# x transposed by its loads, the product written over v, an early filter, a gate that passes through DRAM, and stores from one queue, in a kernel of a gated convolution and a local attention

## The chip, the core and the metric

The kernel runs on one core of a Trainium2 chip. Its engines work side by side and wait for one another through semaphores: TensorE (PE; its weight loads are shown as PEld), VectorE (DVE), ScalarE (ACT), GpSimd (POOL) and SyncE (SP). SP and ACT also issue DMAs; rows marked SPq and ACTq are these. The metric is device time in microseconds (us). Before the change it is 303.62 us, the median of three runs (303.6, 303.62, 306.52).

## The reference

All inputs are bf16. S = 2048 positions, D = 640 channels, H = 32 heads of 20 channels. x is `A_q`, and it serves both branches.

```python
x = A_q
g = sigmoid((x * gate_w).sum(-1, keepdims=True))
# branch a: a long convolution along S, by FFT
k_shift = sum over t of k_pad[:, t:t+S, :] * shift_k[:, 3-t]      # 4 taps
kv = k_shift * v
y  = irfft(rfft(kv padded to 2S) * rfft(ssm_k padded to 2S))[:S] + kv * ssm_D
a  = x * y
# branch b: attention with 8 keys per query, at distances 0, 2, 4 .. 14
q, k, v = split(x @ wqkv)
b  = (softmax(q . k[i - 2w] / sqrt(20)) @ v[i - 2w]) @ wo
out = g * a + (1 - g) * b
```

## The kernel before

**Order of work.** Every piece of work is a Python generator that yields requests (class `Req`: engine, estimated cost, dependencies, PSUM slots). A planner (`Plan.run`) takes them one by one by estimated start time and priority, and the instructions are emitted in that order. So each engine has a fixed order of instructions that rests on the planner's estimates; at run time an engine that waits holds all that stands behind it. PSUM is four slots of two banks. A request with engines "AD" may go to ACT or DVE, whichever the estimates say ends first.

**Layout.** Positions are held by parity: even ones first, then odd ones, so that the dilation of 2 becomes neighbourhood. `xT` is x with channels on the partitions (five blocks of 128).

**Stages, with their names in the profile's rows.**

1. *Loads* (`loads`, L339; all on SP) and small ones on ACT's queue (`heads`, L388): the tap weights `wraw` and the halo of k, both in the tile `early`. x comes as `xS`, and `transposes` (L451) turns it: 80 PE transposes (trx, L458), copied to `xT` by DVE and ACT.
2. *Projections.* `vproj` (L467): 18 units of 10 matmuls (psv, L476), copied to VW. `qkproj` (L507): five column blocks of q and of k, three units of 10 matmuls each (pj, L522), copied to a staging tile `stg`; one to three units make a block's q, three more its k. `fragger` (L541) moves 20-row pieces of `stg` (fragments) by DMA to `qb` and `kb`.
3. *Gate* (`gate`, L487): 160 matmuls of one column (gps, L494), whose weights are strided columns of `xT` in two halves, so that the result stands in the layout of the end. Then an exponential, a reciprocal, and `g_nat` and `omg` (1 - g).
4. *Short convolution* (`conv`, L418): on DVE, four rounds (conv 0 to 3) of 7 operations and a product with v (L443). The product goes to a tile `pv` in another order, from there to DRAM (`kv_d`) once all rounds are done, and back as `kvT` (`kv_back`, L694) with positions on the partitions.
5. *Attention*: eight sets of four heads. Per set five groups of score matmuls (sc, L589), exponentials on ACT (L597, into ETall), 72 products with v (O, L617), normalization on DVE (L626, L629). Three pairs of `kb`/`qb` take turns, so a set's fragments can be moved only when the set three before it has been scored.
6. *Long convolution.* Two steps of a transform (L653 and L669, each followed by copies on ACT or DVE) in two halves of the channels, for the filter (`h`, tile Hs) and for the product (`u`, tile U). `mults` (L750) multiplies them on DVE, with Hs and with Hw, a copy of Hs whose partition halves are swapped by DMA (`swaps`, L734). `inverse1` (L767): ten units of 16 matmuls per half (i, L777), copied to Cm.
7. *Output projection* (`outproj`, L788): oT copies of transposed attention output, then 16 units (op, L810), scaled by `omg` on ACT into bl.
8. *End* (`final`, L841): six units. Each has up to 96 matmuls (i, L859), two copies on ACT (yb, L866), a product and an addition on DVE (L871, L873), and four stores (L876), two issued by SP and two by ACT.

The second swap waits for the last reader of kvT, since its tile takes kvT's place:

```python
yield Req("S", 1.0, outs("h", P) + [ev("p3")] + ([ev("us1")] if P else []))
```

and the stores take turns on two queues:

```python
(nc.sync, nc.scalar)[gg % 2].dma_start(raw(outf, ...), reg[32 * gg:32 * gg + 32])
```

## Time and profile before

| what | value |
|---|---|
| median of three runs | 303.62 us |
| profiled execution: its time, its span | 305.58 us, 303.8 us |
| granted PE clock, mean | 0.844 |
| busy: PE, DVE, ACT | 231.9, 172.5, 177.8 us |
| transposes of x: first start | 10.9 us |
| psv units: first start | 14.2 us |
| gate matmuls | 8.94 us, up to 63.3 us |
| first scores | 63.3 us |
| last O ends | 166 us |
| second swap, issue to landing | 238.5 to 253.2 us |
| last addition on DVE ends | 300.5 us |

A page shows one profiled execution. Busy time is a sum over stages with different limits, so what an edit is worth has to be read in its own stage. Three views are used. The *chain* follows the work that ended last back from the end: each row has its start, its length and what it is (engine, tile, line, number of instructions). The *waits* say who waited for whom: microseconds in total, number of times, the longest. The *timeline* has instructions in order of time; the bracket at a row's end is idle time before it and what ended it ("issue": nothing that the profile shows). The trace also holds a record of every DMA packet with its size and time, and the order of a program's instructions on each engine can be read off the built program.

### The profile page before, as it was taken

How to read it: one execution, taken by the hardware profiler on the slowest of the kernel's cores; microseconds unless marked ns; L12 is line 12 of the kernel's file. 1: busy time of each engine (PE TensorE's matmuls, PEld its weight loads, DVE VectorE, ACT ScalarE, POOL GpSimd, SP SyncE). 2: the span in 40 equal slices, each digit the busy share in tenths (PEclk: the TensorE clock that was granted, in tenths of full speed). 3: DMA queues.
4: the chain of work that ended last, by engine and by line, in shares of the span. 5: the costliest groups of instructions: out<-in, count | busy, mean ns of one | idle time of the engine just before them, and what ended most of it. 6: DMA issues, size and time to landing. Idle time of an engine off the chain costs nothing.

```text
span 303.8 us, 8436 instructions
## 1 busy us (share of the span) xinstructions
PE 231.9 (76%) x3781; PEld 185.7 (61%) x3786; DVE 172.5 (57%) x181; ACT 177.8 (59%) x217; POOL 24.5 (8%) x23
## 2 busy tenths in 40 slices
PE   0499999997988895994888979999999742984210
PEld 0399888965655564563566868889877732973100
DVE  0138999993724334243766999996006656804443
ACT  0146553248368884596977898767756750773240
POOL 9920170000000000001000000000000000000000
PEclk9999999859799799697555999999999795895555
DMA  6982983402166569868993194001990490002343
GB/s 198 321 328 82 371 301 65 127 2 53 25 174 228 147 125 157 139 115 192 281 211 64 25 234 95 2 2 41 202 239 8 100 230 19 2 2 69 77 119 86
DMA packets 36985, 39.92 MB, mean 131 GB/s; under 512 B 23383, under 2 KB 32215, under 8 KB 35798
## 3 DMA queue, kind: packets, MB, share of 16 engines
q1 hardware_dynamic: 34480, 36.78, 48.6%
q10 hardware_dynamic: 2470, 2.62, 3.5%
q8 instruction: 29, 0.48, 0.7%
q14 instruction: 6, 0.05, 0.1%
HBM read 23.49 MB, written 5.24 MB: 95 GB/s over the span
## 4 chain that ended last, share of the span: by engine, by line
PE 58%; DVE 17%; DMA 9%; ACT 6%; SPq 4%; issue 4%; ACTq 1%; DVEq 0%
PE pj L522 14%; PE i L777 9%; PE psv L476 9%; PE op L810 7%; PE O L617 5%; DVE U L269 5%; DVE Hs L269 4%; DMA Hw<-Hs 4%; DMA xS<-in_A_q_dram 3%; PE sc L589 3%; PE gps L494 3%; SPq L563 2%; PE s L669 2%; DMA kb<-stg 2%; DVE qg L871 2%
## 5 line engine op out<-in xcount | busy, mean ns | idle before, releaser
L597 ACT ACTIVATE ETall<-sc 121x912 bf16<-121x912 f32 (+1 forms) x80 | 63.4, 858 | 22.2 <-PE sc L589 21.9
L522 PE MATMUL pj<-xT,Wqk 128*128 128x342 bf16 (+1 forms) x300 | 56.0, 342 | 2.8 <-ACT ETall L597 1.9
L522 PEld LDWEIGHTS <-Wqk 128*128 128x128 bf16 x300 | 30.6, 106 | 20.9 <-issue 3.2
L777 PE MATMUL i<-F,Hs 128*128 128x128 bf16 x160 | 27.2, 251 | 8.6 <-DVE Hs L760 8.6
L777 PEld LDWEIGHTS <-Hs 128*128 128x128 bf16 x160 | 26.0, 183 | 9.0 <-DVE Hs L760 8.8
L267 ACT CAST Cm<-i 128x1024 bf16<-128x1024 f32 x20 | 20.2, 1012 | 17.5 <-PE i L777 17.5
L476 PE MATMUL psv<-Wv,xT 128*121 128x320 bf16 x180 | 28.7, 313 | 1.0 <-DVE xT L269 1.0
L269 DVE CAST U<-s 128x1024 bf16<-128x1024 f32 (+2 forms) x23 | 25.8, 1171 | 6.0 <-PE s L669 3.2
L589 PE MATMUL sc<-qb,kb 31*128 31x114 bf16 x576 | 20.2, 243 | 10.7 <-DMA kb<-stg 3.7
L777 PE MATMUL i<-F,Hw 128*128 128x128 bf16 x160 | 27.1, 252 | 1.3 <-DVE Hw L763 1.3
L777 PEld LDWEIGHTS <-Hw 128*128 128x128 bf16 x160 | 26.0, 183 | 1.5 <-DVE Hw L763 1.5
L267 ACT CAST stg<-pj 128x684 bf16<-128x684 f32 (+1 forms) x21 | 15.6, 745 | 18.7 <-PE pj L522 14.3
L476 PEld LDWEIGHTS <-xT 128*121 128x121 bf16 x180 | 24.9, 142 | 2.5 <-issue 1.2
L267 ACT CAST Hs<-s 128x960 bf16<-128x960 f32 (+1 forms) x25 | 23.1, 994 | 3.1 <-PE s L669 1.8
L589 PEld LDWEIGHTS <-kb 31*128 31x128 bf16 x576 | 11.6, 104 | 20.5 <-issue 14.4
L669 PEld LDWEIGHTS <-G 64*128 64x128 bf16 x512 | 20.9, 103 | 4.4 <-issue 2.7
L269 DVE CAST Hs<-s 128x1024 bf16<-128x1024 f32 (+2 forms) x17 | 19.1, 1152 | 7.6 <-PE s L653 6.1
L810 PE MATMUL op<-wo,oT 128*128 128x512 bf16 (+1 forms) x155 | 22.6, 301 | 0.3
L267 ACT CAST VW<-psv 121x640 bf16<-121x640 f32 x18 | 12.5, 696 | 14.6 <-PE psv L476 14.6
L866 ACT CAST yb<-i 128x960 bf16<-128x960 f32 (+1 forms) x12 | 9.9, 873 | 18.0 <-DVE qg L873 16.8
L810 PEld LDWEIGHTS <-oT 128*128 128x128 bf16 x160 | 16.5, 147 | 5.9
L269 DVE CAST stg<-pj 128x726 bf16<-128x726 f32 (+1 forms) x9 | 8.0, 899 | 21.2 <-PE pj L522 14.6
(57 smaller groups left out, 331.2 us busy)
## 6 DMA issues: line engine op xcount, KB each, us to landing
Hw<-Hs SPq DMA_DIRECT2D x8, 640.0 KB
xS<-in_A_q_dram SPq DMA_DIRECT2D x4, 640.0 KB
kin<-in_A_k_dram SPq DMA_DIRECT2D x2, 1280.0 KB
vin<-in_A_v_dram SPq DMA_DIRECT2D x2, 1280.0 KB
kv_d<-pv SPq DMA_DIRECT2D x4, 640.0 KB
h_lin<-in_A_ssm_k_dram SPq DMA_DIRECT2D x8, 320.0 KB
kvT<-kv_d SPq DMA_DIRECT2D x8, 320.0 KB
qg<-in_A_q_dram SPq DMA_DIRECT2D x4, 640.0 KB
```

The source lines that it names most:

```text
L267: nc.scalar.copy(dst, src)
L269: nc.vector.tensor_copy(dst, src)
L476: nc.tensor.matmul(ps[0:BK, n0 // 320, 0:320], lhsT=xT[:, dt, s0:s0 + BK], rhs=Wv[:, dt, n0:n1], start=(dt == 0), stop=(dt == NDT - 1))
L494: nc.tensor.matmul(gps[64 * hh:64 * hh + 64, t:t + 1], lhsT=raw(a, X0 + 16 * hh + t, [a.ap[0], [32, 64]]), rhs=wg[:, dt:dt + 1], start=(dt ...
L522: nc.tensor.matmul(ps[:, i, 0:n], lhsT=Wqk[:, dt, w, 128 * ft:128 * ft + 128], rhs=xT[:, dt, s0:s0 + n], start=(dt == 0), stop=(dt == NDT ...
L589: nc.tensor.matmul(scs[rg // 2][:, rg % 2, BQ * bb:BQ * bb + BQ], lhsT=kb[r:r + DH + NF, BK * b:BK * b + 128], rhs=qb[r:r + DH + NF, BQ * ...
L597: nc.scalar.activation(st["ET"][0:BK, e, :, 0:BQ * nb], scs[k][0:BK, :, 0:BQ * nb], ACT.Exp, scale=SCALE)
L617: nc.tensor.matmul(O[:, (b - b0) // 6, c0:c0 + 21], lhsT=st["ET"][0:BK, e, hh, BQ * bb:BQ * bb + 128], rhs=VW[0:BK, b, 4 * t + h4, :], sta ...
L669: nc.tensor.matmul(ps[:, c, 160 * jj:160 * jj + 160], lhsT=st["G"][rows, j0 + jj, rr, :], rhs=Am[rows, :, 2 * (j0 + jj) + rr, :], start=(r ...
L777: nc.tensor.matmul(o, lhsT=src[:].rearrange("p q (j c) l -> p c l (q j)", c=2)[:, c, l + il, :], rhs=M[:, k, :], start=(k == 0), stop=(k = ...
L810: nc.tensor.matmul(op[:, n0:n1], lhsT=oT[:, ft].rearrange("p h m a -> p a (h m)")[:, t, :], rhs=wo[:, ft, n0:n1], start=(ft == 0), stop=(f ...
L866: nc.scalar.copy(yb[:, 0:m, 320 * k:320 * k + 320].rearrange("p n (q c) -> p q n c", q=2), pss[k][:, :, 0:160 * m].rearrange("p q (n c) -> ...
```

## The change

Six edits go together.

1. **x.** The four loads of x are now transposing DMAs, straight from DRAM into `xT`. `xS`, the 80 transposes and their copies are gone. Wq and Wk are loaded between the x loads; the tap weights and the halo move from ACT's queue to SP's, behind x. A q or k unit now waits only for the x loads that it reads.
2. **The convolution product** is written over v (`vin`) instead of into `pv`, and each round's part is stored as soon as it is done (`kv_out`). `kv_d` is now a plain position-by-channel array, and `kv_back` reads it in runs of 80 channels.
3. **The filter** `h_lin` has a tile of its own from the start and its loads wait for nothing of the convolution. The tags of several later tiles change places ("H" and "kv"), and the second Hw takes the tile of the first Hs, so the second swap waits for the first half's inverse (`i10`) instead of kvT's last reader.
4. **Gate.** 80 matmuls with contiguous weights; the result, by position, goes to DRAM (`g_scr`) and comes back in the layout of the end by four loads.
5. **Planner.** ACT gets a handicap of 600 (`LEAN_QK`) for the copies of q and k, scores take one PSUM slot at a time, and the estimate of an inverse unit rises. ETall is set to one only in its last 128 columns.
6. **Stores.** All 24 are issued by SP.

In the built program the planner orders the first part anew: 14 psv and 10 pj units stand before the first scores (18 and 7, and the gate, before), and one projection unit instead of three stands before the first inverse units. More copies of q and k go to DVE, and one of the five oT copies to ACT.

```diff
 LAT = {("P", "A"): 230.0, ("P", "D"): 230.0, ("A", "P"): 120.0, ("D", "P"): 120.0, ("A", "D"): 100.0, ("D", "A"): 100.0}
 SWITCH = 110.0
+LEAN_QK = 600.0
...
-        return min((self.start(r, e) + self.cost(r, e), self.start(r, e), e) for e in r.engs)
+        found = []
+        for e in r.engs:
+            s = self.start(r, e)
+            found.append((s + self.cost(r, e) + (r.lean if e == "A" else 0.0), s, e))
+        end, s, e = min(found)
+        return s + self.cost(r, e) if s < INF else INF, s, e
 
     def run(self):
         while self.streams:
...
-    xS = p0.tile([128, 16, D], BF, name="xS", tag="oS")
-    pv = p0.tile([128, 4, 2, 16, 80], BF, name="pv", tag="kv")
+    h_lin = p0.tile([128, 80, 2, 64], BF, name="h_lin", tag="kv")
-    kv_d = dpool.tile([4, 128, 2, 16, 80], BF, name="kv_d")
+    kv_d = dpool.tile([S, D], BF, name="kv_d")
+    g_scr = dpool.tile([S], F32, name="g_scr")
+    g_pos = p0.tile([128, 16], F32, name="g_pos")
...
         def load_x(c):
-            yield from load(f"x{c}", xS[:, 4 * c:4 * c + 4, :], xq4[:, c // 2, 4 * (c % 2):4 * (c % 2) + 4, :], 1900.0)
+            g = yield Req("S", 500.0, (), move=2600.0)
+            nc.sync.dma_start_transpose(xT[:, :, X0 + 512 * c:X0 + 512 * c + 512],
+                                        raw(x2, (1024 * (c % 2) + c // 2) * D, [[2 * D, 512], [1, D]]))
+            mark(f"x{c}", g)
+
+        def load_rows(name, dst, src, r0, r1, deps=(), bg=1500.0):
+            yield from load(name, dst, raw(src, r0 * D, [[16 * D, 128], [1, (r1 - r0) * D]]), (r1 - r0) * 128 * 1280 / 250.0, deps, bg)
...
-            yield from load_rows(f"v{a}", v_[:].rearrange("p n c -> p (n c)"), v2, 8 * a, 8 * a + 8, () if a else [ev("xS")])
-
-        yield from load("ident", ident[:], ca["ident"].ap(), 100.0)
+            yield from load_rows(f"v{a}", v_[:].rearrange("p n c -> p (n c)"), v2, 8 * a, 8 * a + 8, ())
+
         yield from load_x(0)
-        yield from load("Wv", Wv[:], W3[:, :, 2, :], 2400.0)
+        yield from load("Wv", Wv[:], W3[:, :, 2, :], 2600.0)
         yield from load_x(1)
+        yield from load("W0", Wqk[:, :, 0, :], W3[:, :, 0, :], 2600.0)
         yield from load_x(2)
+        yield from load("W1", Wqk[:, :, 1, :], W3[:, :, 1, :], 2600.0)
         yield from load_x(3)
+        yield from load("wraw", wraw.rearrange("p c j -> p (c j)"), raw(A_shift_k, 0, [[0, 128], [1, 4 * D]]), 2200.0)
+        for a, b in ((1, 113), (113, 128)):
+            yield from load(f"halo{a}", halo[a:b].rearrange("p n c -> p (n c)"), raw(k2, (16 * a - 3) * D, [[16 * D, b - a], [1, 3 * D]]), 900.0)
         yield from load_k(0)
-        yield from load("W0", Wqk[:, :, 0, :], W3[:, :, 0, :], 2400.0)
         yield from load_v(0)
-        yield from load("W1", Wqk[:, :, 1, :], W3[:, :, 1, :], 2400.0)
         yield from load_k(1)
         yield from load_v(1)
+        yield from load("ident", ident[:], ca["ident"].ap(), 200.0)
...
-        for q in range(4):
-            yield from load(f"kvD{q}", kv_d[q].rearrange("p c n i -> p (c n i)"), pv[:, q].rearrange("p c n i -> p (c n i)"), 3000.0, [ev("conv")], 1500.0)
-        h_lin = p0.tile([128, 80, 2, 64], BF, name="h_lin", tag="H")
-        st["h"] = h_lin
                 yield from load(f"h{q}{c}", h_lin[32 * q:32 * q + 32, :, c, :],
-                                raw(A_ssm_k, (160 * q + 80 * c) * S, [[64, 32], [S, 80], [1, 64]]), 2100.0, [ev("conv")], 1500.0)
+                                raw(A_ssm_k, (160 * q + 80 * c) * S, [[64, 32], [S, 80], [1, 64]]), 2100.0, (), 1500.0)
+    def kv_out():
+        for a in range(16 // CR):
+            n = CR * a
+            g = yield Req("S", 500.0, [ev(f"conv{a}")], move=2600.0)
+            nc.sync.dma_start(raw(kv_d[0:1, 0:1], n * D, [[16 * D, 128], [1, CR * D]]),
+                              st["vin"][n // 8][:, n % 8:n % 8 + CR, :].rearrange("p n c -> p (n c)"))
+            mark(f"kvD{a}", g)
+
+    def load_G():
+        yield Req("S", 1.0, [ev("conv")])
         G = p0.tile([128, 32, 2, 128], BF, name="G", tag="G")
         st["G"] = G
         for a in range(4):
-            yield from load(f"G{a}", G[:, 8 * a:8 * a + 8], cf["G"].ap().rearrange("p (a r b) -> p a r b", a=32, r=2)[:, 8 * a:8 * a + 8],
-                            1300.0, [ev("conv")], 1500.0)
+            g = yield Req("S", 500.0, [ev("kvD3")], move=2000.0, bg=1500.0, pri=1)
+            nc.sync.dma_start(G[:, 8 * a:8 * a + 8], cf["G"].ap().rearrange("p (a r b) -> p a r b", a=32, r=2)[:, 8 * a:8 * a + 8])
+            mark(f"G{a}", g)
...
-        nc.scalar.dma_start(wraw.rearrange("p c j -> p (c j)"), raw(A_shift_k, 0, [[0, 128], [1, 4 * D]]))
-        for a, b in ((1, 113), (113, 128)):
-            nc.scalar.dma_start(halo[a:b].rearrange("p n c -> p (n c)"), raw(k2, (16 * a - 3) * D, [[16 * D, b - a], [1, 3 * D]]))
...
-        nc.gpsimd.memset(ETall[:], 1.0)
+        nc.gpsimd.memset(ETall[:, :, :, 3 * BQ:], 1.0)
...
-        yield Req("D", 2500.0, [Ev(12000.0)])
+        yield Req("D", 2500.0, [ev("wraw")])
...
-            yield Req("D", c0, [ev(f"k{half}")])
+            yield Req("D", c0, [ev(f"k{half}"), ev("halo113")])
...
-            nc.vector.tensor_tensor(pv[:, :, :, n:n + CR, :].rearrange("p q c n i -> p n (q c) i"),
-                                    pa[:].rearrange("p n (x i) -> p n x i", i=80),
-                                    st["vin"][half][:, r:r + CR, :].rearrange("p n (x i) -> p n x i", i=80), ALU.mult)
+            v_ = st["vin"][half][:, r:r + CR, :]
+            nc.vector.tensor_tensor(v_, pa[:], v_, ALU.mult)
             mark(f"conv{a}", g)
...
-    def transposes():
...
-                        nc.tensor.transpose(tr[:, dd, 128 * k:128 * k + 128], xS[:, 4 * c + k, 128 * (d0 + dd):128 * (d0 + dd) + 128], ident[:, :])
...
-        return [ev(f"xT{c}{d}") for d in (0, 4)]
+        return [ev(f"x{c}")]
...
-        g = yield Req("P", 160 * 28.0, xdeps(3) + xdeps(1) + [ev("vproj")], take=1, mode="c", mm=160)
+        g = yield Req("P", 80 * 28.0, xdeps(3) + xdeps(1) + [ev("vproj")], take=1, mode="f", mm=80)
...
-                a = xT[:, dt, 0:1]
-                for hh in range(2):
-                    nc.tensor.matmul(gps[64 * hh:64 * hh + 64, t:t + 1], lhsT=raw(a, X0 + 16 * hh + t, [a.ap[0], [32, 64]]), rhs=wg[:, dt:dt + 1],
-                                     start=(dt == 0), stop=(dt == NDT - 1), tile_position=(0, 64 * hh), skip_group_check=True)
+                nc.tensor.matmul(gps[:, t:t + 1], lhsT=xT[:, dt, X0 + 128 * t:X0 + 128 * t + 128], rhs=wg[:, dt:dt + 1],
+                                 start=(dt == 0), stop=(dt == NDT - 1), skip_group_check=True)
...
-        nc.scalar.activation(g_nat[:], gps[:], ACT.Exp, scale=-1.0)
+        nc.scalar.activation(g_pos[:], gps[:], ACT.Exp, scale=-1.0)
+        r = yield Req("S", 500.0, [r.done], move=2500.0)
+        nc.sync.dma_start(g_scr[:].rearrange("(t p) -> p t", p=128), g_pos[:])
+        for gg in range(4):
+            r = yield Req("S", 500.0, [r.done], move=200.0)
+            nc.sync.dma_start(g_nat[32 * gg:32 * gg + 32, :], raw(g_scr[0:1], HS * (gg % 2) + 16 * (gg // 2), [[32, 32], [1, 16]]))
+        r = yield Req("D", 200.0, [r.done])
         nc.vector.tensor_scalar(omg[:], g_nat[:], -1.0, 1.0, ALU.mult, ALU.add)
...
-                    g = yield Req("P", 10 * (n / 2.4 + 2.5), xdeps(3) + xdeps(1) + [ev(f"W{w}")], take=1, mode="f", mm=10)
+                    need = {2 * (c // 3) + e for c in (2 * k, 2 * k + 1) for e in range(min(1, (342 * (c % 3) + 341) // 512) + 1)}
...
-                    r = yield Req("AD", n=m, deps=deps, give=g.banks)
+                    r = yield Req("AD", n=m, deps=deps, give=g.banks, lean=LEAN_QK)
...
-                g = yield Req("P", 4 * nb * 28.0 + 30.0, [ev(f"set{t}"), ev("ET")], take=2, mode="s", mm=4 * nb)
-                scs = []
...
+                    g = yield Req("P", 2 * nb * 28.0 + 30.0, [ev(f"set{t}"), ev("ET")], take=1, mode="s", mm=2 * nb)
+                    sc = psum(g, "sc")
...
-        yield Req("G", 1.0, [ev("xS"), ev("conv1")])
+        yield Req("G", 1.0, [ev("conv1"), ev("kvD1")])
...
-        Hs = p0.tile([128, 4, 64, PL], BF, name="Hs", tag="kv")
+        Hs = p0.tile([128, 4, 64, PL], BF, name="Hs", tag="H")
         st[("h", 0)] = Hs
...
-                g = yield Req("S", 500.0, [ev("p2")] + [ev(f"kvD{q_}") for q_ in range(4)], move=1500.0, bg=1500.0)
-                nc.sync.dma_start(st["kvT"][32 * q:32 * q + 32, c].rearrange("p (b n) i -> p b (n i)", b=4),
-                                  kv_d[q, :, c].rearrange("(a b) n i -> a b (n i)", b=4))
+                g = yield Req("S", 700.0, [ev("p2")] + [ev(f"kvD{a}") for a in range(4)], move=2000.0, bg=1500.0)
+                nc.sync.dma_start(st["kvT"][32 * q:32 * q + 32, c], raw(kv_d[0:1, 0:1], 160 * q + 80 * c, [[64 * D, 32], [D, 64], [1, 80]]))
         mark("kvT", g)
...
-        U = p0.tile([128, 4, 64, PL], BF, name="U1", tag="H")
+        U = p0.tile([128, 4, 64, PL], BF, name="U1", tag="kv")
...
-            yield Req("S", 1.0, outs("h", P) + [ev("p3")] + ([ev("us1")] if P else []))
-            Hw = st["p3"].tile([128, 4, 64, PL], BF, name="Hw", tag="Hw") if P == 0 else st["p2"].tile([128, 4, 64, PL], BF, name="Hw", tag="kvT")
+            Hw = st["p3"].tile([128, 4, 64, PL], BF, name="Hw", tag="Hw") if P == 0 else p0.tile([128, 4, 64, PL], BF, name="Hw", tag="H")
             st[("w", P)] = Hw
...
-                    r = yield Req("P", 16 * 64.0 + 30.0, [ev(f"m{P}{c}{l0}")], take=1, mode="f", mm=16)
+                    r = yield Req("P", 16 * 82.0 + 30.0, [ev(f"m{P}{c}{l0}")], take=1, mode="f", mm=16)
...
-        oT = p0.tile([128, NDT, 2, 64, 16], BF, name="oT", tag="H")
+        oT = p0.tile([128, NDT, 2, 64, 16], BF, name="oT", tag="kv")
...
-        yb2 = p0.tile([128, 2, 3, D], BF, name="yb2", tag="H")
+        yb2 = p0.tile([128, 2, 3, D], BF, name="yb2", tag="kv")
...
-                (nc.sync, nc.scalar)[gg % 2].dma_start(raw(outf, (32 * (gg // 2) + gg % 2 + 2 * t0) * D, [[64 * D, 32], [2 * D, m], [1, D]]),
+                nc.sync.dma_start(raw(outf, (32 * (gg // 2) + gg % 2 + 2 * t0) * D, [[64 * D, 32], [2 * D, m], [1, D]]),
                                                        reg[32 * gg:32 * gg + 32])
```

## The prediction

> **What bounds the kernel now.** I read the engine totals, then the chain that ended last, then the table of waits, then single stretches of the timeline. The page:
>
> ```profile
> span 303.8 us, 8436 instructions
> PE 231.9 (76%) x3781; PEld 185.7 (61%) x3786; DVE 172.5 (57%) x181; ACT 177.8 (59%) x217; POOL 24.5 (8%) x23
> PE 58%; DVE 17%; DMA 9%; ACT 6%; SPq 4%; issue 4%; ACTq 1%; DVEq 0%
> ```
>
> PE has most of the chain, but no engine is full for the whole span: the stages end on different things. The chain in order of time (start, length, what):
>
> ```profile
> 1.16 9.72 DMA xS<-in_A_q_dram
> 10.93 1.90 PE trx L458 x16
> 12.86 1.24 DVE xT L269
> 14.22 4.81 PE psv L476 x20
> ...
> 54.39 8.94 PE gps L494 x145
> ...
> 118.16 3.08 DMA kb<-stg
> 121.29 0.56 PE sc L589 x12
> ...
> 242.10 11.11 DMA Hw<-Hs
> 253.33 1.76 DVE Hs L760
> ...
> 278.82 0.97 ACT yb L866
> 279.82 1.17 DVE qg L871
> 281.01 1.17 DVE qg L873
> 282.20 0.38 ACTq L876
> 282.62 0.44 ACTq L876
> 283.28 0.73 issue
> 284.01 0.97 ACT yb L866
> ```
>
> Rows are taken at the full clock (0.844 is granted in the mean). Five places: x arrives late and is turned on PE; the gate is 8.94 us of PE before the first scores (63.3); the score sets then wait for fragments; the second swap leaves PE and DVE idle; and in the tail ACT stands behind its own stores, with a period of 5.19 us (278.82 to 284.01). The waits (total, times, longest) and a PE row of the tail:
>
> ```profile
> ACT yb L866 <- DVE qg L873: 16.8, 5, 3.4
> DVE Hs L760 <- DMA Hw<-Hs: 5.8, 1, 5.8
> ```
> ```profile
> 274.99 1.62 PE L859 MATMUL i<-Cm,T 32*32 32x160 bf16 x128 [1.87 <-issue]
> ```
>
> **Start, up to the first scores.** The 80 transposes, 0.89 us per 16, and their copies go. What x costs instead, no row shows. Below: the four plain x loads, 512 pieces of 1280 B at 58 ns over 16 DMA engines, 1.9 us each. Above: the same elements as 2-byte pieces, 327,680 at the 9 ns of the gate-weight load, 184 us. Between them: runs of 256 B, 2,560 pieces at the 18 ns of the identity's load, 2.9 us. I take 2.9, the row nearest to a load that reads whole runs of 128 columns; the upper end belongs to the slow rival below.
>
> The Trainium skill, "VectorE: DVE Perf Modes", section on the three transpose paths, speaks against the change: it gives the DMA path 1309 ns for 128x128, which for 20 blocks is an estimate of 26 us a load. "Advanced Engine Details and Errata", section X-Bar Transpose (TRN2), says instead that such DMAs run at about 90% of a plain copy. No row here decides between them; by the first page's figure the sum below would come to about 367 us, by the second's to what I forecast.
>
> Before, the tap weights (38.6 us of engine time, 2.4 us over 16) and the halo rode ACT's queue beside x; now they stand behind x on SP's. First data came 1.7 us after its issue. Adding in queue order from 2.4 us: x0 5.3, Wv 8.2 (2.3, and 0.5 for ACT's small loads), x1 11.1, Wq 13.4, x2 16.3, Wk 18.6, x3 21.5, taps 23.9, halo 25.7, k 28.8; about 1.2 more until a consumer starts. PE starts at 9.4, not 10.9, and has no wait for x3 (23 us). The new order has 14 psv units (1.36 us) and 10 pj units (1.47) before the first scores: 9.4 + 19.0 + 14.7 = 43.1, against 63.3. ETall cannot be set before the halo is read, near 37; its memset took 6.35 us for 7,520 columns, so 1.7 for 2,048, and the exponentials are not held. The gate comes later: 80 contiguous matmuls at the transposes' 56 ns (same 128x128 weights) are 4.5 us, against 8.94.
>
> **What is late next: DVE.** The convolution's first operation, at 25.7 before, waits for taps, halo, k and two staging copies now: 31.4. Conv 0 takes 12.4 us, conv 1 12.1, one staging copy 0.9 (a bank is held until then), 16 operations of 1.49 and the first two sets' normalizations (2.7 each) follow: conv 3 ends near 86, against 83.5. Writing the product over v costs the same 1.49. The third block's k staging (0.9) stands behind it on DVE, and behind that on SP four kb fragments (0.75 each) and about 2.5 us to land: the fourth set's scores start at 92.7 instead of 106.7. PE and ACT can serve three sets by then (first at 43, second at 67 after the gate, third near 79; a set is 8.6 us of exponentials), so DVE sets this date: 14 us gained. Bounds: 5, if PSUM banks held for DVE stop PE as well, and 20, where the second set already stands.
>
> From the fourth set on the order keeps its shape: the fifth set's last kb fragment still stands behind two q fragments that wait for the fourth set's scores (118.16 above). The lead stays 14 us up to the last O, at 166 before. More staging copies on DVE and the filter loaded early (four stage-1 units go into that gap) I put at zero: ACT has 76 us of work in 110 there.
>
> **Through DRAM.** Product stores: same size, free of conv's end. Reading them back now takes 16,384 pieces of 160 B; between 13 ns (the filter's 128 B) and 18 ns (256 B) that is 13.3 to 18.4 us, against 12.6 now. The last piece landed at 163.1, first use is 172.1: 9 us of cover, and the cost is what exceeds it. The gate's store, 2,048 pieces of 4 B at 9 ns, is 1.2 us, 7.4 at 58 ns; its values are used some 80 us later. But its store waits on SP for DVE's reciprocal, with the fifth set's q fragments behind it, and the four loads add 0.5 us of SP each: zero to 3 us. Zero taken.
>
> **Output projection and first inverse.** One projection unit instead of three now stands before the first inverse units, and ACT makes one of the five oT copies: PE waits for the first two products (1.74 each). Dates: op 199.0 to 200.4, products ready 201.5, ten inverse units of 1.31 to 214.7, fifteen of 1.40 to 235.7, against 233.6. Cost 2.1.
>
> **Second swap.** Its tile no longer waits for the last reader of kvT but for the first inverse, so it is issued near 215, beside 21 us of projection; it needs 13 (238.54 to 253.2). DVE's 5.8 us wait goes; next is DVE's own cast at 247.5. If the clock stays at full speed, up to 0.8 more.
>
> **Tail.** ACT no longer queues behind the stores. DVE's two operations, 2.35 us, would be the period, but PE is next: 128 matmuls run in 1.6 us and then wait for issue, 3.46 us from page to page (274.99, 278.45). By that, units 1 to 5 end on PE at 275.7, 278.8, 280.0, 283.0 and 283.4; adding ACT's 1.82 and DVE's 2.35 in turn, the last addition ends at 288.65 instead of 300.53: 11.9. SP issues four stores one after the other where two queues shared them, 0.85 later at the end. Net 11.0; 8 if store bandwidth binds (384 pieces of 96 ns over 16 engines are 2.3 us per unit).
>
> **Sum**, against the profiled execution's span: 303.8 - 14 + 2.1 - 5.8 - 11.0 = 275.1. Its execution took 305.58, so 276.9; the median, 303.62, lies 2.0 below that execution: 275.
>
> **Rivals.** *The early gain is lost:* DVE's convolution, SP's in-order waits and the fragments give back most of the 14, and swap and tail alone stay: 303.6 + 2.1 - 5.8 - 11.0 = 289. For it: DVE starts conv 5.7 us later; against: the set dates above.
> *The tail stays slow:* instruction issue or stores keep some 4 us of period: 281. For it the 1.87 rows; against, the 3.46 pitch.
> *PE and ACT gain more:* sets at the pace of exponentials, 268.
> *Slower: the transposing loads.* The change does turn x in the DMA, but in short pieces. If a load writes 32 bytes per partition at a time, 20,480 pieces at the 9 ns that the smallest take are 11.5 us. Everything behind x waits four times the excess: 4 x (11.5 - 2.9) = 34, so 275 + 34 = 309, slower by 1.8%. It decides from 2.9 + 28.5/4 = 10 us a load. For it: the smallest pieces' price; against: the x data here are whole 1280 B rows.
>
> **How the numbers follow.** Forecast 0.55 (270 to 282), early gain lost 0.14, slow tail 0.10, more gain 0.09, slow transposes 0.12 (300 to 340, a quarter of it within 1%). A measurement of this kernel tells about 1% from no change. Faster by over 1%: 0.88; slower by over 1%: 0.09; within: 0.03. Range 264 to 294: it takes in the bounds 5 and 20 of the lead and the first three rivals, and leaves out the slow transposes.
>
> **What would show it.** First psv near 9.5 and no trx rows; first scores near 43, fourth set near 93; gps about 4.5 us; no wait of DVE Hs on Hw<-Hs; ACT yb waits for PE, not for qg, and yb rows 2.4 to 3.5 us apart. It is wrong if psv units wait for x beyond 25 us, if scores wait for kb beyond the dates given, or if the stores' landing sets the end.

## The result, and the profile after

The changed kernel takes **283.19 us** (median of 281.92, 282.81, 283.58 and 284.1) against 305.07 us for the kernel before on the same chip: a ratio of 0.927, with a 95% interval of 0.918 to 0.936. The forecast was 275.0 with a range of 264 to 294. Ratios, here and below, compare the executions in the faster of two states that the record tells apart, while a median takes in all of them, so a ratio can differ a little from the quotient of two medians. The profiled execution took 281.92 us, its span is 280.1 us, and the sum had said 275.1.

The head of the page of the changed kernel: span, busy times, and the shares of the chain by engine.

```profile
span 280.1 us, 8105 instructions
PE 224.8 (80%) x3622; PEld 179.5 (64%) x3626; DVE 175.6 (63%) x186; ACT 169.0 (60%) x204; POOL 20.2 (7%) x23
...
PE 59%; DVE 12%; ACT 10%; DMA 8%; issue 5%; SPq 3%; ACTq 1%; DVEq 0%
```

No engine's busy time moved by more than 9 us (PE 231.9 to 224.8, ACT 177.8 to 169.0, DVE up by 3), and the span fell by 23.7: most of it is waiting. Where it went, the chain tells. Its rows have start, length and what; lines are those of the changed kernel.

```profile
0.74 2.92 SPq L355
...
3.72 5.90 DMA Wv<-in_B_wqkv_dram
9.66 7.12 PE psv L481 x40
...
44.90 1.49 PE pj L532 x10
46.39 0.34 PE sc L597 x16
...
63.85 1.98 PE gps L497 x80
...
96.81 11.31 DMA g_scr<-g_pos
108.19 0.82 SPq L509
...
115.01 0.79 PE s L660 x8
...
117.53 0.91 PE sc L597 x14
...
186.46 1.75 DVE Hs L766
...
239.07 1.76 DVE Hs L766
...
265.31 1.62 PE i L865 x118
266.94 1.83 issue
```

Read it beside the rows of before: the transposes are gone and PE starts at 9.66; the first scores start at 46.3 instead of 63.3; the gate takes 1.98 us instead of 8.94. The 11.11 us of `Hw<-Hs` are gone from the chain. In their place stands something new, 11.31 us of `g_scr<-g_pos`: the gate's store to DRAM, with four filter units (s, L660) and then the fifth set's scores behind it. The chain doesn't say whether the store itself or what lies between holds them; the experiments ask that. The waits of the changed kernel (total, times, longest) say the same of swap and tail: no wait on `Hw<-Hs` is left, DVE now waits for the projection's end, and the yb copies wait for PE.

```profile
DVE U L277 <- ACT bl L820: 7.3, 1, 7.3
...
ACT yb L872 <- PE i L865: 4.5, 4, 1.3
```

Step by step, from the dates of the two profiled executions (lead of the changed kernel; the spans differ by 23.7 us):

| stretch | forecast | before | after | gain |
|---|---|---|---|---|
| start to last O | +14 | 166.96 | 156.55 | +10.4 |
| to DVE's first product | 0 | 31.79 | 29.91 | +1.9 |
| to the last projection matmul | -2.1 | 34.85 | 38.58 | -3.7 |
| to the second half's first product | +5.8 | 19.73 | 14.03 | +5.7 |
| to the last addition | +11.9 | 47.20 | 35.68 | +11.5 |
| to the end | -0.85 | 3.27 | 5.35 | -2.1 |

The forecast of the sum is missed by 5.0 us: 3.6 up to the last O, 1.6 in the projection, 1.2 at the very end and 0.4 in the tail, less the 1.9 that came for nothing. The 1.9 and the 3.7 belong together: with one projection unit instead of three ahead of the inverse, DVE's first product comes sooner and the last projection matmul later. From the last O to that matmul it is 66.6 us before and 68.5 after, a cost of 1.9 where the forecast had 2.1.

### The profile page after: what moved, and what is told of

It reads as the page before. It is cut to its first block, busy times and chain, and to the rows that moved or that the text cites. A ratio compares the mean times of both kernels' runs of the same rounds, so it can differ in the third digit from the quotient of the medians.

```text
span 280.1 us, 8105 instructions
## 1 busy us (share of the span) xinstructions
PE 224.8 (80%) x3622; PEld 179.5 (64%) x3626; DVE 175.6 (63%) x186; ACT 169.0 (60%) x204; POOL 20.2 (7%) x23
## 4 chain that ended last, share of the span: by engine, by line
PE 59%; DVE 12%; ACT 10%; DMA 8%; issue 5%; SPq 3%; ACTq 1%; DVEq 0%
PE pj L532 15%; PE i L783 10%; PE psv L481 10%; PE op L816 7%; ACT ETall L604 5%; DVE U L277 5%; PE s L676 5%; DMA g_scr<-g_pos 4%; PE sc L597 4%; PE O L624 3%; ACT U L275 3%; DMA Wv<-in_B_wqkv_dram 2%; PE i L865 2%; DMA h_lin<-in_A_ssm_k_dram 2%; DVE Hs L277 2%
## 5 line engine op out<-in xcount | busy, mean ns | idle before, releaser
L532 PE MATMUL pj<-xT,Wqk 128*128 128x342 bf16 (+1 forms) x300 | 54.7, 335 | 2.0 <-DVE stg L277 0.9
L532 PEld LDWEIGHTS <-Wqk 128*128 128x128 bf16 x300 | 30.3, 104 | 19.5 <-issue 2.4
L277 DVE CAST stg<-pj 128x726 bf16<-128x726 f32 (+1 forms) x18 | 16.1, 894 | 35.1 <-PE pj L532 33.5
L481 PEld LDWEIGHTS <-xT 128*121 128x121 bf16 x180 | 25.6, 143 | 11.5 <-POOL qb L423 7.5
L783 PE MATMUL i<-F,Hs 128*128 128x128 bf16 x160 | 28.6, 263 | 2.9 <-DVE Hs L766 2.9
L783 PE MATMUL i<-F,Hw 128*128 128x128 bf16 x160 | 28.4, 264 | 2.1 <-DVE Hw L769 2.1
L597 PE MATMUL sc<-qb,kb 31*128 31x114 bf16 x576 | 23.7, 240 | 8.0 <-ACT ETall L604 5.8
L275 ACT CAST Hs<-s 128x960 bf16<-128x960 f32 (+1 forms) x24 | 22.4, 1009 | 8.0 <-PE s L660 5.5
L597 PEld LDWEIGHTS <-kb 31*128 31x128 bf16 x576 | 14.1, 104 | 17.9 <-issue 17.0
L277 DVE CAST Hs<-s 128x1024 bf16<-128x1024 f32 (+2 forms) x18 | 20.5, 1152 | 7.2 <-PE s L660 5.0
L676 PEld LDWEIGHTS <-G 64*128 64x128 bf16 x512 | 22.0, 107 | 4.3 <-issue 2.7
L624 PEld LDWEIGHTS <-ETall 121*128 121x128 bf16 x576 | 17.2, 100 | 4.6 <-issue 2.9
L624 PE MATMUL O<-VW,ETall 121*128 121x21 bf16 x576 | 18.0, 176 | 2.4 <-ACT ETall L604 1.9
```

The lines of the kernel that those rows point to most:

```text
L275: nc.scalar.copy(dst, src)
L277: nc.vector.tensor_copy(dst, src)
L481: nc.tensor.matmul(ps[0:BK, n0 // 320, 0:320], lhsT=xT[:, dt, s0:s0 + BK], rhs=Wv[:, dt, n0:n1], start=(dt == 0), stop=(dt == NDT - 1))
L532: nc.tensor.matmul(ps[:, i, 0:n], lhsT=Wqk[:, dt, w, 128 * ft:128 * ft + 128], rhs=xT[:, dt, s0:s0 + n], start=(dt == 0), stop=(dt == NDT ...
L597: nc.tensor.matmul(sc[:, hh, BQ * bb:BQ * bb + BQ], lhsT=kb[r:r + DH + NF, BK * b:BK * b + 128], rhs=qb[r:r + DH + NF, BQ * b:BQ * b + BQ] ...
L624: nc.tensor.matmul(O[:, (b - b0) // 6, c0:c0 + 21], lhsT=st["ET"][0:BK, e, hh, BQ * bb:BQ * bb + 128], rhs=VW[0:BK, b, 4 * t + h4, :], sta ...
```

## The experiments

Each kernel was timed beside the kernel before on the same chip. Since chips and hours differ by up to 1.3% (the kernel before had medians of 304.28 to 308.22), ratios to before are compared, and dates inside the profiles.

| run | median, us | ratio to before | 95% interval |
|---|---|---|---|
| changed kernel | 283.19 | 0.927 | 0.918 to 0.936 |
| alt_stores | 291.45 | 0.958 | 0.950 to 0.967 |
| old_swap | 288.37 | 0.946 | 0.939 to 0.953 |
| gate_late | 282.10 | 0.927 | 0.919 to 0.935 |
| old_gate | 279.87 | 0.910 | 0.898 to 0.922 |
| gate_pool | 285.96 | 0.930 | 0.923 to 0.937 |
| op3 | 283.28 | 0.921 | 0.915 to 0.928 |
| plain_x | 284.14 | 0.925 | 0.917 to 0.932 |
| pe_transposes | 284.31 | 0.923 | 0.916 to 0.930 |
| store_rows | 280.74 | 0.915 | 0.911 to 0.919 |
| gate_sbuf | 281.77 | 0.919 | 0.915 to 0.923 |
| pet_gs | 276.83 | 0.903 | 0.899 to 0.907 |
| order_alike | 279.88 | 0.921 | 0.916 to 0.926 |

And the dates that the readings below use (us from the start of the profiled execution):

| | before | after | store_rows | old_gate | gate_sbuf | pe_transposes | pet_gs | order_alike |
|---|---|---|---|---|---|---|---|---|
| first scores | 63.3 | 46.3 | 46.7 | 46.2 | 46.7 | 49.1 | 50.5 | 52.3 |
| convolution starts | 25.7 | 33.1 | 33.5 | 33.0 | 33.5 | 28.8 | 30.3 | 30.6 |
| convolution ends | 83.5 | 88.8 | 89.2 | 93.6 | 93.9 | 82.6 | 88.6 | 90.7 |
| fourth set | 106.7 | 98.4 | 98.8 | 101.0 | 103.0 | 100.2 | 96.7 | 98.2 |
| fifth set | 117.4 | 117.5 | 113.5 | 113.7 | 117.6 | 115.8 | 109.8 | 111.3 |
| its second group of scores | 124.7 | 121.3 | 117.3 | 117.8 | 122.1 | 121.5 | 116.6 | 118.3 |
| sixth set | 133.3 | 128.9 | 125.4 | 125.4 | 129.6 | 128.9 | 124.2 | 126.7 |
| last O | 166.96 | 156.55 | 154.36 | 153.79 | 157.19 | 156.90 | 151.89 | 154.36 |

A set's date is that of its first score matmul. Before, the fifth set's first group then stood still until 121.3 for a k fragment, so the second group compares better there.

### The tail: stores on two queues again

```diff
-                nc.sync.dma_start(raw(outf, ...), reg[32 * gg:32 * gg + 32])
+                (nc.sync, nc.scalar)[gg % 2].dma_start(raw(outf, ...), reg[32 * gg:32 * gg + 32])
```

> The changed kernel with the stores of the end shared between SP and ACT again; all else stays. If ACT standing behind its own stores was the period of the tail (5.19 us before, against rows 2.4 to 3.5 us apart now), the net 9.4 us that the tail gained go again: about 292.5 us, 290 to 295, with ACT's yb rows waiting for DVE's qg. If the tail became shorter for another reason (the stores' landing, the order of the matmuls), ACT's stores cost little: 282 to 285.

Measured 291.45 us, as the first theory has it. The chain of this run shows the old loop: two stores on ACT, the copy, the two operations on DVE, and 5.47 us from copy to copy (270.70 to 276.17).

```profile
274.08 0.37 ACTq L882
...
274.50 0.44 ACTq L882
...
276.17 0.97 ACT yb L872
...
277.17 1.17 DVE qg L877
...
278.37 1.17 DVE qg L879
```

From the second half's first product to the last addition it takes 47.93 us, against 35.68: 12.2 us for the loop. From the last addition to the end it takes 3.0 us, against 5.35: stores by one queue cost 2.35 us there, not 0.85. When the last addition ends in the changed kernel (274.75), SP is still issuing the four stores of the unit before, until 275.60; its own four are issued from 275.71 to 277.71. Here, with two queues, the last issue ends 0.9 us after the addition (288.38), against 3.0.

### The second swap where it was

```diff
-            ... ([ev("i10")] if P else []))
+            ... ([ev("us1")] if P else []))
-            Hw = ... else p0.tile([128, 4, 64, PL], BF, name="Hw", tag="H")
+            Hw = ... else st["p2"].tile([128, 4, 64, PL], BF, name="Hw", tag="kvT")
```

> The changed kernel with the second swap where it was before: its tile in the place of kvT, waiting for kvT's last reader. If the swap was on the path, it is issued some 4.9 us after the projection's end (225.05) and lands 14.7 us later, near 244.7, where DVE's first product of the second half now starts at 239.07: 5.6 us later, 288.8 us (287.5 to 290). If something else would end as late anyway (DVE's own casts, the clock), less than 2 us: 283 to 285.

Measured 288.37. The wait of before is back in the table of waits, and the stretch from the projection's end to DVE's product takes 20.0 us (226.48 to 246.51) instead of 14.0.

```profile
DVE Hs L766 <- DMA Hw<-Hs: 6.1, 1, 6.1
```

### The gate's way through DRAM

Four runs ask what the 11.31 us row costs. The first moves only the loads that read the gate back:

```diff
-            r = yield Req("S", 500.0, [r.done], move=200.0)
+            r = yield Req("S", 500.0, [r.done, ev("frags")], move=200.0)
```

> The changed kernel with the four loads that bring the gate back from DRAM moved behind the last fragment; the store of the gate stays where it is. If SP's wait for the 11.3 us landing of that store is what holds the fifth set's fragments, SP has the wait of 2.7 us and the issue of 0.8 us less in front of them, and the fifth set starts 2 to 3.5 us earlier: 279.5 to 281.5 us. If those fragments waited for their staging copies or for the scores of the set before anyway, nothing changes: 282.5 to 284.

Measured 282.10: nothing, and the theory of SP's wait falls. In the timeline of PE of this run (the bracket is the idle time before, and what ended it) the four filter units still wait until 116.1, for GpSimd's addition, and that waits for the last filter load; the fifth set's scores stand behind them.

```profile
116.13 1.64 PE L660 MATMUL s<-F,h_lin 64*128 64x128 bf16 x24 [2.86 <-POOL h_lin L687]
118.01 0.61 PE L660 MATMUL s<-F,h_lin 64*128 64x128 bf16 x8 [0.25 <-ACT Hs L275]
118.66 0.84 PE L597 MATMUL sc<-qb,kb 31*128 31x114 bf16 x16
```

The second takes the way through DRAM out, and takes the old 160 matmuls back:

```diff
-                nc.tensor.matmul(gps[:, t:t + 1], lhsT=xT[:, dt, X0 + 128 * t:X0 + 128 * t + 128], ...)
+                for hh in range(2):
+                    nc.tensor.matmul(gps[64 * hh:64 * hh + 64, t:t + 1], lhsT=raw(a, X0 + 16 * hh + t, [a.ap[0], [32, 64]]), ...)
...
-        nc.sync.dma_start(g_scr[:]...)
-        (four loads from g_scr)
```

> The changed kernel with the gate as it was before: 160 matmuls on strided halves, no way through DRAM. Two things move: PE has about 7 us more of gate matmuls (8.94 against 1.98 us) between the first and the second set, and SP loses the wait of 2.7 us and five DMA issues. If DVE's convolution sets the date of the fourth set, the 7 us are hidden and the time falls by 1 to 3 us: 280 to 282. If PE is the bound there, the 7 us count: 286 to 290.

Measured 279.87, ratio 0.910. The second set starts 4.8 us later (72.6 for 67.8), so the 7 us of PE are not hidden as I had it, and yet the last O is 2.8 us earlier: without the store, the sets after the fourth more than make it up. This is not the store alone: in this run's order on PE one projection unit instead of three stands right ahead of the fourth set, and two filter units instead of four ahead of the fifth. The planner also put three projection units ahead of the first inverse here; the stretch from the first product to the last projection matmul took 34.84 us, 3.7 less, of which 1.4 are lost again in the stretch before it (31.3 us from the last O to the first product, against 29.9). The third gives the store and the loads to GpSimd's queue:

```diff
-        r = yield Req("S", 500.0, [r.done], move=2500.0)
-        nc.sync.dma_start(g_scr[:].rearrange("(t p) -> p t", p=128), g_pos[:])
+        r = yield Req("G", 500.0, [r.done])
+        nc.gpsimd.dma_start(g_scr[:].rearrange("(t p) -> p t", p=128), g_pos[:])
```

> The changed kernel with the gate's store and its four loads issued by GpSimd instead of SP, the loads behind the last fragment; the matmuls stay. If the store's 2,048 pieces, on SP's queue, hold up the filter loads behind them, and through these the fifth set (four filter units stand ahead of its scores on PE and waited until 114.94 for the last filter load and GpSimd's addition), the fifth set starts 4 to 6 us before the 117.5 of the changed kernel. The planner also puts three projection units instead of one before the first inverse units here, which took 34.8 us instead of 38.6 where it did so with the old gate. Together 275.5 us, 273 to 278. If the filter loads take as long without the store in their queue, only the order's part is left: 279 to 281.

Measured 285.96, a clear miss: the fifth set starts at 120.0. So it is not SP's queue alone. The packet records show something else: fragments' pieces of 4104 B that start between 103 and 110 us take 330 ns in the mean without such a store (old_gate 328), but 563 in the changed kernel, 707 in gate_late and 1127 here, one of them 4.0 us. (GpSimd's store stands in the records as 32 packets of 256 B, 435 ns each, 7 ns for every 4 B.) So the fragments' pieces are slow behind the 4-byte writes on whichever queue they stand. The fourth run changes nothing but the size of the pieces, in an otherwise identical program:

```diff
-        nc.sync.dma_start(g_scr[:].rearrange("(t p) -> p t", p=128), g_pos[:])
+        nc.sync.dma_start(g_scr[:].rearrange("(p t) -> p t", p=128), g_pos[:])
```

> The changed kernel with one difference: the gate's store writes each partition's 16 values as one piece of 64 B (128 pieces) instead of 2,048 pieces of 4 B. The gates then stand at the wrong positions in DRAM, so the output is mixed with the wrong gates; every instruction and its order stay. If the 4-byte pieces are what clogs the DMA engines (the store took 11.3 us to land, and fragments of 4104 B behind it 670 to 960 ns a piece instead of 320 to 350), the store lands in some 2 us, the filter loads behind it come 4 to 5 us earlier, and the fifth set starts near 113 instead of 117.5: 278.5 us, 277 to 280.5. If it is the way through DRAM itself or the queue's order, whatever the pieces, 282.5 to 284.

Measured 280.74, ratio 0.915; the span falls from 280.1 to 276.5. The 128 pieces start within 0.2 us (98.08 to 98.27), the store has landed 1.5 us after its issue, the 4104-byte pieces behind take 330 ns, and the last filter load is issued at 104.72 instead of 109.52: the fifth set starts at 113.5, not 117.5.

```profile
104.72 5.04 DMA h_lin<-in_A_ssm_k_dram
...
110.92 0.80 PE s L660 x8
...
113.45 0.91 PE sc L597 x14
```

In this pair the profiled span differs by 3.6 us (1.2% of before in the ratios, whose intervals overlap slightly). Up to the last O it is 2.2 us (156.55 becomes 154.36), or 2.6 with the start that was 0.4 later: most of the shortfall of 3.6 there, not all of it. The rest of the span's 3.6 comes behind the last O, at a granted clock of 0.863 in the mean of the execution against 0.852, and is not shown to be the store's.

### The projection in front of the inverse

```diff
-   r = yield Req("P", 16 * 82.0 + 30.0, [ev(f"m{P}{c}{l0}")], ...)
+   r = yield Req("P", 16 * 82.0 + 30.0, [ev(f"m{P}{c}{l0}")] + ([ev("bl1")] if P == 0 else []), ...)
```

> The changed kernel with the first inverse held until three projection units stand before it on PE (one before); nothing else is moved. If PE's waits for DVE's first products are what made the stretch from the first projection to the last 38.6 us long, it falls to about 35 us and the time by 3.7: 279.5 us, 278.5 to 281. If the length comes from the rows themselves (clock, banks), less than 1 us: 282 to 284.

Measured 283.28, ratio 0.921, inside the interval of the changed kernel. In the profile the stretch falls from 38.58 to 36.78 us (189.90 to 226.68): 1.8 us, half of what I expected for this stretch (bl1 is the copy of the second projection unit; with it the planner puts three units ahead). old_gate, gate_pool and pet_gs, with 34.8 to 35.0 here, also order the last oT transposes otherwise, and lose part of it in the stretch before: from the last O to the last projection matmul they take 66.1, 68.8 and 67.4 us, op3 66.3 and the changed kernel 68.5. Nor does the level time say that the edit gives nothing: in this execution the store took 12.2 us to land and the last O ends 3.8 us later than in the changed kernel, and behind it the span is 3.4 us shorter (120.2 against 123.6).

### What turning x in the DMA costs, and what it is worth

```diff
-            nc.sync.dma_start_transpose(xT[:, :, X0 + 512 * c:X0 + 512 * c + 512],
-                                        raw(x2, (1024 * (c % 2) + c // 2) * D, [[2 * D, 512], [1, D]]))
+            nc.sync.dma_start(xT[:, :, X0 + 512 * c:X0 + 512 * c + 512],
+                              raw(x2, 512 * c * D, [[4 * D, 128], [512, NDT], [1, 512]]))
```

> The changed kernel with x loaded by plain DMAs of the same size into the same tile, so that x is not turned and all that follows from it is computed from other numbers. It shows what the turning itself costs. SP is held 15.5 us by the issue of the four transposing loads and should be held some 2 us here, so taps, halo and k come up to 5 us earlier and the convolution starts near 29 instead of 33.1. If the later dates hang on the convolution, 280 to 281 us; if the fifth set waits for the filter anyway, the gain is lost again there: 282 to 283.5. If turning in the DMA is dear beside that (slower data as well), below 279.

Measured 284.14, ratio 0.925: no difference. SP is held far less (first the timeline of SP's issues in the changed kernel, then in this run):

```profile
10.66 4.67 SPq L355 DMA_TRANSPOSE xT<-in_A_q_dram  x1
15.38 0.58 SPq L350 DMA_DIRECT2D Wqk<-in_B_wqkv_dram  x1
16.01 5.30 SPq L355 DMA_TRANSPOSE xT<-in_A_q_dram  x1
```
```profile
8.59 0.55 SPq L355 DMA_DIRECT2D xT<-in_A_q_dram  x1
9.18 0.69 SPq L350 DMA_DIRECT2D Wqk<-in_B_wqkv_dram  x1
9.91 1.19 SPq L355 DMA_DIRECT2D xT<-in_A_q_dram  x1
```

k is issued at 14.4 instead of 23.0, and still the convolution starts only 1.2 us sooner (31.97), not 4. DVE's timeline of this run says why: two staging copies stand ahead of it on DVE and wait for PE.

```profile
28.29 0.91 DVE L277 CAST stg<-pj 128x726 bf16<-128x726 f32 x1 [4.59 <-PE pj L532]
31.14 0.91 DVE L277 CAST stg<-pj 128x726 bf16<-128x726 f32 x1 [1.94 <-PE pj L532]
31.97 1.15 DVE L444 TENSOR_TENSOR pa<-early,wl 128x1920 bf16<-128x1920 bf16 x1
```

So the turning costs nothing that this pair can show. Then the other way round, x turned on PE as before, in the changed kernel (its tile, 80 transposes and copies back, the identity loaded first, the convolution's v waiting for them):

```diff
-            nc.sync.dma_start_transpose(xT[...], ...)
+            yield from load(f"x{c}", xS[:, 4 * c:4 * c + 4, :], xq4[...], 1900.0)
...
+    plan.add(transposes(), 1)
```

> The changed kernel with x loaded plainly and turned on PE as before, with the 80 transposes and their copies; the new order of loads and all other edits stay. If the start is on the path up to the last O, PE's first psv comes some 4 us later and 80 transposes of 4.5 us and copies on DVE come back: the sets start 5 to 9 us later, 287 to 291 us. If only the later sets' dates count, which DVE and SP set, the gain of the start is lost before the fifth set: 283 to 285.

Measured 284.31, ratio 0.923: level. The first scores come at 49.1, only 2.8 us after the changed kernel and still 14 us ahead of before. PE's first psv is not 4 us later, as I expected, but at 9.41 against 9.66: in the new order of loads, without the tap weights and the halo beside it, x reaches PE's first transpose at 6.1 us, not at 10.9. But this comparison is disturbed by the gate. Here its store is issued just ahead of the fourth set's k fragments, and in the chain a fragment takes 12.29 us to land:

```profile
87.88 12.29 DMA kb<-stg
...
100.22 0.76 PE sc L609 x7
```

So both were compared again without the store. The gate's matmuls take columns 16 apart, a partition then holds 16 neighbouring positions, and four copies from tile to tile put the partitions in order:

```diff
-                nc.tensor.matmul(gps[:, t:t + 1], lhsT=xT[:, dt, X0 + 128 * t:X0 + 128 * t + 128], ...)
+                nc.tensor.matmul(gps[:, t:t + 1], lhsT=raw(a, X0 + t, [a.ap[0], [16, 128]]), ...)
...
-        nc.sync.dma_start(g_scr[:]...)
-        (four loads from g_scr)
+            r = yield Req("S", 500.0, [r.done, ev("frags")], move=200.0)
+            nc.sync.dma_start(g_nat[32 * gg:32 * gg + 32, :], g_pos[p0_:p0_ + 63:2, :])
```

> The changed kernel with the gate's 80 matmuls on columns 16 apart, so that a partition holds 16 neighbouring positions, and four copies from tile to tile (128 pieces of 64 B) behind the last fragment in place of the way through DRAM. No store, no wait of SP for it, and the planner puts five projection units instead of one before the first inverse units. Fifth set near 112 instead of 117.5 (5 us), and up to 3.7 us less between the first projection and the last; 80 strided matmuls cost up to 2.5 us more on PE ahead of the second set, hidden as the 7 us of the old gate were. 276 us, 274 to 279. If the fifth set is held by the filter loads with or without the store, 279.5 to 282.

Measured 281.77, ratio 0.919, not clear of the changed kernel and in the range of the second expectation. Its condition holds too: the fifth set starts at 117.6, and PE waits for the last filter load and GpSimd's addition as before.

```profile
115.86 1.53 PE L660 MATMUL s<-F,h_lin 64*128 64x128 bf16 x24 [2.88 <-POOL h_lin L687]
```

Up to the last O nothing is gained (157.19 against 156.55); the 3.2 us of the span come behind it. The price was mine to see: the strided matmuls take 4.89 us in the chain, the second set starts 5.1 us later and the fourth 4.6, and even the convolution ends 5.1 us later, because DVE's normalizations stand between its operations and wait for PE.

```profile
64.55 4.89 PE gps L498 x80
```

With x turned on PE in that kernel (the edits of pe_transposes and gate_sbuf together):

```diff
-            nc.sync.dma_start_transpose(xT[...], ...)
+            yield from load(f"x{c}", xS[:, 4 * c:4 * c + 4, :], xq4[...], 1900.0)
```

> The kernel of the run gate_sbuf, with x turned on PE as before. It asks what the transposing loads are worth where the gate's store no longer holds a set: with that store, turning x on PE ended level with the changed kernel, but there the store stood ahead of the fourth set's fragments (12.3 us to land) and not of the fifth's. If the start is on the path of the later sets, 4 to 8 us above gate_sbuf. If the sets from the fourth on hang on the convolution and on SP, within 1.5 us of it, or even below, since the convolution started at 28.8 there against 33.1.

Measured **276.83 us, ratio 0.903**, the fastest of all: below gate_sbuf by 1.7%, and below the changed kernel, with intervals that do not meet. It is also 2.0% below pe_transposes, from which it differs by the gate alone and the order that the planner then makes: the last O ends 5.0 us sooner. The first scores come 3.8 us later than in gate_sbuf, the fourth set 6.3 us sooner. In PE's order one projection unit stands ahead of the fourth set instead of three, and no filter unit ahead of the fifth. The last run gives that order to the kernel with the transposing loads, by two numbers of the planner:

```diff
-        g = yield Req("P", 80 * 28.0, ...)
+        g = yield Req("P", 80 * 60.0, ...)
...
-    plan.add(qkproj(), 3)
+    plan.add(qkproj(), 4)
```

> The kernel of the run gate_sbuf (x by transposing loads, gate from tile to tile), with two numbers of the planner changed (the priority of the q and k units 4 instead of 3, the estimate of a gate matmul 60 ns instead of 28) so that PE's order from the fourth set on is the one of the run pet_gs: one projection unit instead of three ahead of the fourth set, no filter units ahead of the fifth. If that order made pet_gs faster than gate_sbuf (276.83 against 281.77 us, fifth set 109.8 against 117.6), this one ends level with pet_gs: 275.5 to 278, fourth set near 97 and fifth near 110. If the loading of x made it, through the convolution that starts at 33.5 instead of 30.3, the sets from the fourth on come 3 us later than there and the time is 279 to 281.

Measured 279.88, ratio 0.921: in the range of the second expectation, and level with gate_sbuf. By the ratios, then, the order gives nothing. The dates lie between the two expectations. Its profiled execution, the fastest of its six at 277.2, has the fourth set at 98.2 and the last O at 154.36: against gate_sbuf it gains 4.8 and 2.8 us by the order, and stays 1.5 and 2.5 us behind pet_gs. In the profiles, then, the order goes with a little more than half of the 5.3 us between the two kernels at the last O. What makes the rest, whether the transposing loads do, and why the medians are further apart than the profiles (1.8% in the ratios, 1.4 us in the spans), stays open.

## Why the prediction was right or wrong

**The sign and the range were right**, but 283.19 lies 1.2 us outside the band of the main case (270 to 282): the range held because it allowed for a lead of 5 to 20 us, not because the way to the last O was right. Two of the large terms are shown one by one. The swap: 5.8 forecast, 5.7 in the dates, 6.0 when undone. The tail's loop: 11.9 forecast, 11.5 in the dates, 12.2 when undone; the pauses of PE's issue that I put in its place are there (1.83, 1.90 us).

**The start: right in its first dates, wrong in its reason.** PE started at 9.66 (9.4 forecast). The first scores came at 46.3, not 43.1: 15 psv units stand ahead of them, not 14 (1.36), and the first twelve matmuls run at half the pace, 0.27 us from one to the next against 0.135 after 12.8 us, which makes the first four units 1.5 us longer. But the prediction put the 14 us down to x arriving late and being turned on PE. With x turned on PE again the first scores are 2.8 us later, of a lead of 17. The rest comes with the new order: of the loads, by which PE's first psv starts at 9.41 instead of 14.22 even so (4.8 us), and on PE, where the gate (8.94 us) stands behind the first scores; the fewer psv units are made up for by more pj units (16 and 9 there, 18 and 7 before). None of the 2.8 us reaches the end of that run's span (280.1 us both). So the agreement at the first scores is partly luck. The early filter, the product over v and the planner's numbers were not taken out one by one, so which edit gives the 10 us at the last O stays open.

**The price of a transposing load was nearly right.** The 10,240 pieces of 256 B take 18 ns in the median and 20.3 in the mean, 3.25 us a load over 16 engines (2.9 forecast from 18 ns; 2.1 for the plain load of plain_x). The Trainium skill, "VectorE: DVE Perf Modes", section on the three transpose paths, gives 1309 ns for 128x128, an estimate of 26 us a load; in this trace the pieces of all four loads lie between 2.2 and 22.8 us, which refutes it for loads of this size. "Advanced Engine Details and Errata", section X-Bar Transpose (TRN2), with some 90% of a plain copy, is nearer: 2.1 of 3.25 is 65% here. What I left out is the issue: SP is held 2.62 to 5.30 us by each, against 0.55 to 1.19. Taking that away (plain_x) gained nothing here, since the convolution then waits for staging copies.

**The gate's matmuls** were put at 4.5 us, at the transposes' 56 ns each, and took 1.98, or 25 ns each. **Reading the product back** took 19.9 us of engine time, above the 13.3 to 18.4 forecast, and ended at 159.3 us, before PE's first use at 161.0: a cost of nothing, as taken.

**"DVE sets this date" was the step that failed for the fourth set** (98.4, not 92.7). DVE's side came 1.7 us late: the convolution ended at 88.8 (86 forecast), and the last of the four k fragments had landed at 94.35 by the trace's semaphores. The other 4.0 us are PE's own order:

```profile
89.64 3.01 PE L532 MATMUL pj<-xT,Wqk 128*128 128x342 bf16 x10 [0.91 <-DVE stg L277]
93.14 5.32 PE L532 MATMUL pj<-xT,Wqk 128*128 128x342 bf16 x30
98.38 0.58 PE L597 MATMUL sc<-qb,kb 31*128 31x114 bf16 x24
```

Four projection units stand between the third set's last scores and the fourth set, the first held by a PSUM bank that waits for DVE's copy (88.68 in the chain), and the granted clock is 0.50 from 87.9 to 94.7 (3.01 us for the first ten matmuls, 1.49 at full clock). I had followed DVE and SP to the date and not PE's own order. The runs with one projection unit right ahead of the set instead of three start it 7.4 to 8.1 us after the convolution's end (old_gate, order_alike, pet_gs), those with three 9.1 to 9.6 (gate_sbuf, the changed kernel, store_rows). pe_transposes, where the convolution ends 6.2 us sooner and the fourth set comes no sooner, proves nothing here, because the gate's store holds its k fragment.

**"Zero to 3 us, zero taken" was the step that failed for the gate.** I bounded the store by its engine time: 2,048 pieces at 9 ns, 1.2 us. It took even less of that (15.2 us over 16 engines, 0.95). But its landing took 11.3, and what follows on the DMA engines is slow too. The wait that I looked for, SP's, is not what counted (gate_late): the filter loads are, and the filter units that stand ahead of the fifth set, which the planner could put there because the filter is loaded early. That edit I had put at zero as well. The lead over before shrinks from 8.3 us at the fourth set to 3.4 at the fifth set's second group and 4.4 at the sixth set, and then grows to 10.4 at the last O, so "the lead stays" was wrong in both directions. What made the last sets faster than before (17.7 us from the sixth to the eighth, 22.4 before) no run takes apart.

**The projection** cost 3.7 instead of 2.1 from DVE's first product on, but 1.9 from the last O on, so this term was about right. **The last stores** cost 2.1 instead of 0.85: I counted the last unit's own issues and not that SP still stood in those of the unit before. Of the 8.2 us between 275.0 and 283.19, the other 3.2 come from profile to median: before, the median lay 2.0 below the profiled execution, and I took that over; after, it lies 1.3 above it.

The rivals: "the early gain is lost" (289) describes what happened for 3.6 us of it. "Slow transposes" needed 10 us a load and got 3.25.

## What to carry to other kernels

Before a large gain at the start is counted, take the edit out alone and see whether the dates downstream follow: here 17 us at the first scores were 10 at the last O, and in none of the pairs was x turned by its loads ahead of x turned on PE. Bound a DMA not only by its engine time but by its landing, and ask what passes the same engines next; a store of single 4-byte values can be worth a rearrangement on chip (pe_transposes to pet_gs, 0.923 to 0.903, in an order that changed with it). And where a planner decides the order, read the built order of every engine up to the date that you predict, the unit right in front of it above all.

## What the runs showed of the hardware

- **A store of 4-byte pieces to DRAM slowed the DMAs behind it.** 2,048 values of 4 B, 7 ns each in the records, took 11.3 us to land (12.2 in op3), and 4104-byte copies from tile to tile behind them 563 to 1127 ns instead of 330, whichever queue issued the store. 128 pieces of 64 B with the same 8 KB did neither (landed after 1.5 us, 330 ns). The Trainium skill, "DMA: Bandwidth & Descriptors", section Specifications, says that transfers below 512 B are done by read-modify-write; a reason of that kind would fit the 4-byte pieces, but 64 B are below that bound too and went well, so the bound alone does not tell the case.
- **Matmuls with strided weights were slower.** The 80 gate matmuls took 1.98 us with 128 neighbouring columns as weights (25 ns each), and 4.89 with columns 16 apart (61 ns); the old 160, with 64 columns 32 apart, 8.94 (56 ns). The granted clock is not the reason: with columns 16 apart they took 5.06 us from first to last at 1.00 (order_alike) and 5.11 at 0.76 (pet_gs), against 2.14 at 1.00 in the changed kernel.
- **A transposing DMA held the queue that issued it longer**, 2.92, 2.62, 4.67 and 5.30 us here, against 0.55 to 1.19 for plain loads of the same bytes.
